# Hash attention before a SwiGLU block: all hash products in 32 columns, signs written once and spread, the late ones moved behind the row sums

## The chip, the core and the metric

The kernel runs on one NeuronCore of one Trainium2 chip. The metric is the device time of one execution in microseconds (us). The core has a matrix engine (TensorE, "PE" in the profile, with its weight loads as "PEld"), VectorE ("DVE"), ScalarE ("ACT"), GpSimd ("POOL") and SyncE ("SP"). Each engine carries out its own instructions in order. DMAs are issued by SP, ACT and POOL queues ("SPq", "ACTq", "POOLq") and carried by 16 shared DMA engines.

## What is computed

```python
# q, k, v: (4, 8, 768, 64), proj: (64, 6)
q_bits = (einsum('bhsd,dk->bhsk', q, proj) > 0)
k_bits = (einsum('bhsd,dk->bhsk', k, proj) > 0)
q_bucket = sum(q_bits * 2**arange(6), axis=-1)       # k_bucket likewise
mask = q_bucket[:, :, :, None] == k_bucket[:, :, None, :]
scores = where(mask, q @ k.T / 8, -1e9)
attn = softmax(scores)
x = (attn @ v).transpose(0, 2, 1, 3).reshape(3072, 512)
g = x @ w_gate                                       # (512, 1536)
out = (g * sigmoid(g) * (x @ w_val)) @ w_out         # (1536, 512)
```

Two tokens attend to each other only if the signs of all six hash products agree.

## The kernel before

**Pairs and units.** The 32 heads are handled two at a time: a pair n (0 to 15) is one batch and two heads, and head h of the pair lies in partitions 64h to 64h+63. A pair has two halves of 384 query columns, and a half has six chunks c of 128 keys. The main loop (L729) takes one half per turn: six times `score` (L448), then six times `attend` (L460), with `add` (L478) summing the exponentials on VectorE between scores.

**The mask as a product.** For each head, `score` adds two products in PSUM (L451 to L456): the one of the fp32 operands `T["k"]`, `T["q"]`, for both heads, and then the one of the bf16 operands `bits["k"]`, `bits["q"]` (tiles `kb`, `qb`), again for both heads. The bits are the signs of the hash products. The ones of k are multiplied by 2^34, with a constant row, so that a key with any other sign falls by a huge number and its exponential is zero. The operand rows of head 0 are partitions 0 to 63, those of head 1 are 64 to 127.

**The steps that prepare a pair.** `front(n)` (L369) returns a list of steps for pair n. For pairs 0 to 4 these are four transposes on TensorE, each with a ScalarE copy (`transpose`, L372), and four hash products (`hash_bits`, L392), each with a full 128-column weight `hash_w` in which the 32 hash columns stand twice, at columns 0 and 64. Each gives all 128 rows, so one ScalarE sign (L387) writes both heads, and for k one VectorE multiplication (L389) follows. `prepare_pair` (L717) runs steps, and `finish(rest)` runs the multiplications they leave behind. For pairs 1 to 4 the transposes of pair n+1 are issued in the first half of pair n, the two k products in the second half behind the scores (L750), and the two q products behind the attends (L760). The next instructions of TensorE are the scores of pair n+1.

For pairs 5 to 15 the transposes are done on VectorE, and `hash_blocks` (L398) issues four products of 32 columns into four groups of 32 PSUM partitions, with weights `hash_w[:, 0:32]`. A sign is then taken twice, once to partitions 0 to 31 and once to 64 to 95, and for k each is multiplied separately. These steps are `chores` (L769), handed out one for each unit of size of the feed-forward pieces (`atoms`, L780): size 1 for an up product (L625), size 2 for a down product (L690). The first chore of a second half is nothing, the second is `hash_blocks`, so that two up products stand between it and what is ahead of it.

**The row sums.** `total(n)` (L489) multiplies the sums of exponentials by `ones` in four 32-column products (L500, tile `sum`), takes a reciprocal on VectorE (L508), and issues eight SP transfers (L513) of 32 x 384 fp32 that spread it over partitions. `norm` (L518) then scales `xT`. For pairs 0 to 3 `total` is issued in the next pair, behind its second score; for later pairs at the end of the second half.

**The SP queue.** At the end of a second half `load(n + 2)` (L757) issues q, k and v of that pair on SP. v has two buffers, so the one of pair n+2 waits for the attends of pair n.

**The weights.** During the first quarter of the time VectorE and ScalarE turn the feed-forward weights from doubles to fp32 (`narrow`, L285) and form sums of blocks (`form`, L310). `prepare_on` hands these out four and three steps per half. GpSimd loads the words (L263) and moves formed blocks to and from DRAM (L308, L318, L320, L329).

Of the kernel before, what the change touches and what calls it, by code (L numbers as in the profile page):

```python
# [8 lines left out]
FP32 = mybir.dt.float32  # L9
# [3 lines left out]
ALU = mybir.AluOpType  # L13
AF = mybir.ActivationFunctionType
# [4 lines left out]
def kernel(  # L19
# [11 lines left out]
    nc = tc.nc  # L31
# [38 lines left out]
    def bank(name):  # L70
        return banks.tile([P, 512], FP32, tag="ps", name=name)
# [68 lines left out]
    HR = 16  # L140
    assert NBITS + 1 <= HR and 2 * HR == BLOCK
    rules = wraw.tile([P, PIECE, 2], I32, tag="words", name="rules").rearrange("p f w -> p (f w)")
    rules = rules.bitcast(FP32)[:, 0 : 2 * P].rearrange("p (x r) -> p x r", r=P)

    nc.gpsimd.memset(rules[:, 0, :], -(2.0**-120))
    nc.gpsimd.memset(rules[:, 1, :], 0.0)
    groups = rules.rearrange("p x (g r) -> p x g r", r=HR)
    nc.gpsimd.memset(groups[:, 0, :, NBITS : NBITS + 1], 1.0)
    for h in range(2):
        g = groups[:, 1, h * D // HR + h, :]  # L150
        nc.gpsimd.memset(g[:, 0:NBITS], OFF / 2)
        nc.gpsimd.memset(g[:, NBITS : NBITS + 1], -NBITS * OFF / 2)
    nc.vector.tensor_tensor(rules, rules, ident.unsqueeze(1).to_broadcast([P, 2, P]), op=ALU.mult)
    columns = konst.tile([P, 2], FP32, tag="columns", name="columns")
    nc.vector.tensor_reduce(out=columns, in_=rules, axis=AX.X, op=ALU.add)
    nudge, times_k = (columns[:, x : x + 1] for x in range(2))

    hash_w = konst.tile([P, P], FP32, tag="hash", name="hash")
    nc.vector.memset(hash_w, 0.0)
    for h in range(2):  # L160
        rows = slice(h * D, (h + 1) * D)
        nc.vector.tensor_copy(hash_w[rows, h * HR : h * HR + NBITS], two_proj[rows, :])
    nc.vector.tensor_copy(hash_w[:, D : D + BLOCK], hash_w[:, 0:BLOCK])
    ones = konst.tile([P, BLOCK], FP32, tag="ones", name="ones")
    nc.gpsimd.memset(ones, 1.0)

# [4 lines left out]
    for i in range(RING):  # L171
        t = konst.tile([P, 2, AW], FP32, tag=f"A{i}", name="A")
        nc.gpsimd.memset(t[:, :, HQ:AW], 1.0)
        ring.append(t)

# [176 lines left out]
    def prepare_on(n):  # L354
        for _ in range(n):
            next(preparing, None)
# [12 lines left out]
    def front(n):  # L369


        def transpose(name, half):  # L372
            if (name, n) not in T:
                T[name, n] = opnd.tile([P, S], FP32, tag=name + "T", name=name + "T")
            ps = bank("tps")
            for i in range(CH):
                nc.tensor.transpose(ps[:, i * P : (i + 1) * P],
                                    raws[name, n][:, half * CH + i, :, :].rearrange("p h d -> p (h d)"),
                                    ident)
            nc.scalar.copy(T[name, n][:, half * HQ : (half + 1) * HQ], ps[:, 0:HQ])  # L380

        bits["q", n] = sides["q", n % 2]
        bits["k", n] = sides["k", n % 2]

        def sign(name, half, to, ps):
            o = bits[name, n][to, half * HQ : (half + 1) * HQ]
            nc.scalar.activation(o, ps, AF.Sign, bias=nudge[to])  # L387
            if name == "k":
                return lambda: nc.vector.tensor_scalar(o, o, scalar1=times_k[to], scalar2=None,  # L389
                                                       op0=ALU.mult)  # L390

        def hash_bits(name, half):  # L392
            ps = bank("hps")
            nc.tensor.matmul(ps[:, 0:HQ], hash_w, T[name, n][:, half * HQ : (half + 1) * HQ],  # L394
                             start=True, stop=True)
            return [sign(name, half, slice(0, P), ps[:, 0:HQ])]

        def hash_blocks():  # L398

            tile_ = bank("hps")  # L400
            for i, (name, half) in enumerate((name, half) for name in "kq" for half in range(2)):
                nc.tensor.matmul(tile_[i * BLOCK : (i + 1) * BLOCK, 0:HQ],  # L402
                                 hash_w[:, 0:BLOCK], T[name, n][:, half * HQ : (half + 1) * HQ],
                                 start=True, stop=True)

            def evict(name, half):
                i = 2 * (name == "q") + half
                ps = tile_[i * BLOCK : (i + 1) * BLOCK, 0:HQ]
                for to in (0, D):
                    scale = sign(name, half, slice(to, to + BLOCK), ps)  # L410
                    if scale:
                        more.append(scale)

            more = []
            return [lambda at=at: evict(*at) for at in
                    (("k", 0), ("k", 1), ("q", 0), ("q", 1))] + [lambda: [f() for f in more] and None]

        def transpose_blocks(name):
            T[name, n] = opnd.tile([P, S], FP32, tag=name + "T", name=name + "T")
            nc.vector.transpose(T[name, n], raws[name, n].rearrange("p c h d -> p (c h d)"))  # L420

        if n > NP:

            return [lambda name=name: transpose_blocks(name) for name in "qk"] + [hash_blocks]
        order = [("k", 0), ("k", 1), ("q", 0), ("q", 1)]
        turns = [lambda x=x: transpose(*x) for x in order]
        hashes = [lambda x=x: hash_bits(*x) for x in order]
        if n == 0:
            return [turns[0], turns[2], hashes[0], hashes[2], turns[1], hashes[1], turns[3],
                    hashes[3]]  # L430
        return turns + hashes


    units = [(n, half, c) for n in range(len(pairs)) for half in range(2) for c in range(NCH)]
# [282 lines left out]
    def prepare_pair(count):  # L717
        for _ in range(count):
            rest.extend(f for f in steps.pop(0)() or [] if f)

    def finish(todo):
        while todo:
            todo.pop(0)()

    prepare_pair(4)
    finish(rest)
    N = len(units)
    credit = 0.0
    for u in range(0, N, NCH):  # L729
        n, half, _ = units[u]  # L730
        gating = u >= LATE
        if u == MOVE:
            progress["late"] = True
            for t in late_ring:
                nc.gpsimd.memset(t[:, :, HQ:AW], 1.0)
        for c in range(NCH):
            score(u + c)
            if u == 0 and c in (0, 1, 2, 4):
                prepare_pair(1)
                finish(rest)  # L740
            if c == 1 and half == 0 and 0 < n <= NP:
                total(n - 1)
            if c:
                add(u + c)
        if n <= NP:
            finish(waiting)
        if not gating and half == 0:
            steps = front(n + 1)
        if not gating and u > 0:
            prepare_pair(2)  # L750
        for _ in range(1 if u else 2):
            scale_ahead()
        for c in range(NCH):
            attend(u + c)
        if not gating:
            scale_ahead()
        if half == 1 and n + 2 < len(pairs):  # L757
            load(n + 2)
        if not gating:
            prepare_pair(2 if u > 0 else 4)  # L760
        finish(first)
        finish(rest)
        prepare_on(0 if u == LATE else 4)
        if half == 1 and n >= NP:
            total(n)
        prepare_on(0 if LATE - NCH <= u <= LATE else 3)
        if not gating:
            continue
        chores = []  # L769
        if n + 1 < len(pairs):  # L770
            if half == 0:
                steps = front(n + 1)
                chores = [None, steps.pop(0), None, steps.pop(0)]
            else:
                chores = [None, steps.pop(0)]

        credit += 14 if n < 2 * NP else 15.75
        end = True
        part = 0
        while atoms and (credit > 0 or not end):  # L780
            size, atom, end = atoms.pop(0)
            credit -= size
            atom()
            part += size
            if part >= 11 or u + NCH == N and part >= 6:
                finish(waiting)
                if u + NCH == N:
                    finish([first.pop(0) for _ in range(min(2, len(first)))])
            if 5 < part < 14 if u == LATE else part < 9:
                prepare_on(size)  # L790
            if 6 < part < 11 or u == LATE and part > 10:
                scale_ahead()
            for _ in range(size):
                if chores:
                    step = chores.pop(0)
                    chores.extend(step and step() or [])
        while chores:
            step = chores.pop(0)
            chores.extend(step and step() or [])
# [34 lines left out]
```

The softmax here doesn't subtract the row's maximum and nothing guards it: scores larger than these inputs give would overflow.

## Time and profile before

| | |
|---|---|
| median of 3 runs | 1008.99 us (1008.4 to 1009.31) |
| the profiled execution | 1007.17 us |
| its span, first to last instruction | 1005.4 us |
| PE busy | 999.8 us (99%) |
| DVE busy | 574.7 us (57%) |
| ACT busy | 417.4 us (42%) |
| hash products, 128 columns (L394) | 40 of them |
| hash products, 32 columns (L402) | 88 of them |
| signs of 32 x 384 (L387) | 88, mean 569 to 573 ns |
| v loads on SP (L81) | 16 of 384 KB, median 3.3 us from issue to landing |

An fp32 product stands in the trace as two matmul instructions. The kernel's TensorE instructions are pipelined, so a row's mean duration of a matmul (490 ns for 384 columns) is longer than the distance to the next one; the chain of waits, which lays instructions end to end, gives the distances. The span falls into two parts. Up to some 119.5 us there is attention of pairs 0 to 4 with the weights prepared beside it; from there on attention and feed-forward products alternate (the weights are all prepared by about 290 us), and attention ends at about 802 us.

### The profile page before, as it was taken

The page shows a single profiled execution, that of the slowest core. Times are in us where ns is not written, and L with a number is a line of the kernel's source. Part 1 is how long each engine was busy: PE and PEld are TensorE (multiplying, and loading weights), DVE is VectorE, ACT ScalarE, POOL GpSimd, SP SyncE. Part 2 cuts the span into 40 slices and gives each one's busy share as a digit, 9 for nine tenths or more (in the row PEclk, how much of TensorE's full clock was granted, in tenths as well). Part 3 has the DMA queues.
Part 4 walks back from the last instruction along what each step waited for, and adds up shares of the span by engine and source line. Part 5 has one row for each costly group of instructions (what it writes and reads, how often), then busy time and mean ns, then how long its engine had stood idle before and what let it go on. Part 6 is the DMA issues. An engine that isn't in the chain of part 4 may idle for free.

```text
span 1005.4 us, 12486 instructions
## 1 busy us (share of the span) xinstructions
PE 999.8 (99%) x4597; PEld 603.9 (60%) x4597; DVE 574.7 (57%) x919; ACT 417.4 (42%) x921; POOL 98.7 (10%) x192
## 2 busy tenths in 40 slices
PE   9999999999999999999999999999999999999998
PEld 4444455555576775555557776555555787555687
DVE  4788898887883624556464543545557342435421
ACT  7777457575424215335351323435444201222200
POOL 2222132231000000000000000000000000111000
PEclk9999999999999999999999999999999999999999
DMA  7777495886213032433331304242122011323101
GB/s 229 200 257 228 145 243 156 229 279 169 76 39 78 22 95 67 101 97 92 95 105 28 72 17 115 76 102 84 54 85 78 22 37 63 105 76 113 32 27 37
DMA packets 120029, 106.21 MB, mean 106 GB/s; under 512 B 89024, under 2 KB 103360, under 8 KB 119968
## 3 DMA queue, kind: packets, MB, share of 16 engines
q0 software_dynamic: 19104, 73.28, 22.8%
q1 hardware_dynamic: 100064, 31.94, 14.0%
q8 instruction: 36, 0.59, 0.3%
q10 hardware_dynamic: 800, 0.20, 0.1%
q14 instruction: 25, 0.20, 0.1%
HBM read 81.79 MB, written 17.30 MB: 99 GB/s over the span
## 4 chain that ended last, share of the span: by engine, by line
PE 89%; DVE 7%; SPq 2%; issue 1%; DMA 1%; DVEq 0%; ACT 0%
PE up L544 42%; PE po L544 21%; PE sc L455 12%; PE av L469 10%; SPq L513 2%; DVE acc L487 1%; PE sum L500 1%; DVE wo L508 1%; PE hps L402 1%; DMA wo<-wo 1%; DVE room L294 1%; PE hps L394 1%; DVE room L326 0%; DVE room L349 0%; DVE xT L520 0%
## 5 line engine op out<-in xcount | busy, mean ns | idle before, releaser
L544 PE MATMUL up<-xT,room 128*128 128x384 f32 x768 | 263.7, 490 | 0.4 <-DVE xT L520 0.4
L544 PEld LDWEIGHTS up<-xT,room 128*128 128x128 f32 x768 | 144.2, 190 | 110.3 <-issue 15.4
L544 PE MATMUL up<-xc,room 128*128 128x384 f32 x576 | 197.4, 487 | 0.0
L455 PE MATMUL sc<-qT,kT 64*128 64x384 f32 x768 | 160.3, 494 | 0.0
L544 PEld LDWEIGHTS up<-xc,room 128*128 128x128 f32 x576 | 109.7, 191 | 76.0 <-ACT hid L607 0.2
L548 DVE TENSOR_TENSOR c<-c,up 128x384 f32<-128x384 f32 x72 | 39.8, 553 | 179.7 <-PE up L544 178.5
L487 DVE TENSOR_TENSOR acc<-acc,A 128x768 f32<-128x768 f32 x128 | 122.7, 958 | 15.4 <-ACT A L458 2.6
L308 POOL DMA_DIRECT2D room<-ram x96 | 51.9, 541 | 717.9 <-PE up L544 710.3
L458 ACT ACTIVATE A<-sc 128x384 f32<-128x384 f32 x256 | 105.4, 505 | 4.9 <-PE sc L455 4.7
L679 ACT COPY o<-po 128x256 f32<-128x256 f32 x48 | 17.9, 372 | 196.5 <-PE po L544 196.5
L455 PEld LDWEIGHTS sc<-qT,kT 64*128 64x128 f32 x768 | 68.0, 187 | 50.7 <-issue 43.3
L469 PE MATMUL av<-A,vraw 128*64 128x384 f32 (+1 forms) x512 | 88.2, 487 | 0.0
L530 ACT ACTIVATE th<-c 128x384 f32<-128x384 f32 x72 | 37.6, 523 | 110.9 <-DVE c L531 83.4
L548 DVE TENSOR_TENSOR o<-o,po 128x256 f32<-128x256 f32 x36 | 15.1, 421 | 111.6 <-PE po L544 82.4
L458 ACT ACTIVATE room<-sc 128x384 f32<-128x384 f32 x128 | 54.4, 495 | 33.6 <-PE sc L455 33.6
L544 PE MATMUL po<-wo,hid 128*128 128x256 f32 x288 | 66.9, 382 | 0.0
L544 PE MATMUL po<-wo,room 128*128 128x256 f32 x288 | 66.6, 381 | 0.2 <-DVE room L548 0.2
L544 PE MATMUL po<-room,hid 128*128 128x256 f32 x288 | 66.1, 380 | 0.0
L607 ACT COPY c<-up 128x384 f32<-128x384 f32 x72 | 34.4, 478 | 74.5 <-PE up L544 74.3
L455 PE MATMUL sc<-qb,kb 64*128 64x384 bf16 x384 | 65.2, 323 | 0.0
L469 PEld LDWEIGHTS av<-A,vraw 128*64 128x64 f32 x512 | 36.8, 137 | 46.0 <-issue 45.4
L544 PEld LDWEIGHTS po<-wo,hid 128*128 128x128 f32 x288 | 54.2, 190 | 12.0 <-issue 4.9
(109 smaller groups left out, 998.3 us busy)
## 6 DMA issues: line engine op xcount, KB each, us to landing
room<-ram POOLq DMA_DIRECT2D x48, 512.0 KB, 4.7
room<-ram POOLq DMA_DIRECT2D x48, 384.0 KB, 3.9
vraw<-in_v_dram SPq DMA_DIRECT2D x16, 384.0 KB, 3.3
ram<-room POOLq DMA_DIRECT2D x12, 512.0 KB, 4.7
out_dram<-o SPq DMA_DIRECT2D x48, 128.0 KB, 1.7
room<-in_moe_w_out_dram POOLq DMA_DIRECT2D x10, 512.0 KB, 6.7
qraw<-in_q_dram SPq DMA_DIRECT2D x48, 96.0 KB, 3.1
hid<-in_moe_w_gate_dram POOLq DMA_DIRECT2D x9, 512.0 KB, 6.2
```

Source lines behind the costliest of these rows:

```text
L294: nc.vector.scalar_tensor_tensor(out=wi, in0=hi, scalar=-(1 << 31), in1=wi, op0=ALU.bitwise_and, op1=ALU.bitwise_or)
L308: nc.gpsimd.dma_start(places[k % 2][:, PARTS[go], :], ram[k % NG][:, PARTS[go], :])
L455: nc.tensor.matmul(sc[h], x["k", n][rows, ks], x["q", n][rows, qs], start=start, stop=not start)
L458: nc.scalar.activation(weights(u)[:, h, 0:HQ], sc[h], AF.Exp, scale=SCALE)
L469: nc.tensor.matmul(ps[h * D : (h + 1) * D, 0:width], raws["v", n][:, h, c, :], a[:, h, 0:width], start=c == 0, stop=c == NCH - 1)
L487: nc.vector.tensor_tensor(acc[n, half], acc[n, half], a[:, :, 0:HQ], op=ALU.add)
L513: nc.sync.dma_start(t[at : at + BLOCK, half, :], r[g : g + BLOCK, :])
L530: nc.scalar.activation(th, g, AF.Tanh, scale=0.5)
L544: nc.tensor.matmul(ps, a, x, start=start and i == 0, stop=i == len(pairs_) - 1, skip_group_check=True)
L548: nc.vector.tensor_tensor(o, a, b, op=op)
L607: nc.scalar.copy(tile_of(g, spot), c)
L679: nc.scalar.copy(o, c)
```

## The change

1. `hash_w` has 32 columns instead of 128; every hash product goes through `hash_blocks(todo, own)`, which puts up to four of them side by side in one PSUM tile.
2. A sign is taken once, to partitions 0 to 31. `spread` then makes partitions 64 to 95: for k by two VectorE multiplications over all columns of `todo` (high from low, then low in place), for q by a VectorE copy in pair 0 and by one transfer on the SP queue in all other pairs.
3. The scale for k becomes two columns; three of the bits tiles are cleared by GpSimd at the start, as partitions 32 to 63 and 96 to 127 are no longer written.
4. Pairs 1 to 4: one step with all four products stands behind the second score of the second half of the pair before; its `spread` is run by the `finish(rest)` behind the attends and behind `load(n + 2)`.
5. Pairs 5 to 15: the four products are issued right behind `total(n)`; the four signs and `spread` are chores.
6. Pair 0: k and q of the first half are hashed together before the first score, those of the second half together behind the third score.

```diff
-    hash_w = konst.tile([P, P], FP32, tag="hash", name="hash")
+    hash_w = konst.tile([P, BLOCK], FP32, tag="hash", name="hash")
...
-    nc.vector.tensor_copy(hash_w[:, D : D + BLOCK], hash_w[:, 0:BLOCK])
...
+    for t in (sides["k", 0], sides["q", 0], sides["q", 1]):
+        nc.gpsimd.memset(t, 0.0)
...
+        def hash_blocks(todo, own):
             tile_ = bank("hps")
+            for i, (name, half) in enumerate(todo):
+                nc.tensor.matmul(tile_[i * BLOCK : (i + 1) * BLOCK, 0:HQ], hash_w,
+                                 T[name, n][:, half * HQ : (half + 1) * HQ],
                                  start=True, stop=True)
+            low, high = slice(0, BLOCK), slice(D, D + BLOCK)
+
+            def sign(i, name, half):
+                nc.scalar.activation(bits[name, n][low, half * HQ : (half + 1) * HQ],
+                                     tile_[i * BLOCK : (i + 1) * BLOCK, 0:HQ], AF.Sign, bias=nudge)
+
+            def spread():
+                for name in "kq":
+                    hs = [half for x, half in todo if x == name]
+                    b = bits[name, n][:, hs[0] * HQ : (hs[-1] + 1) * HQ]
+                    if name == "k":
+                        for to, times in ((high, times_k[1]), (low, times_k[0])):
+                            nc.vector.tensor_scalar(b[to], b[low], scalar1=times, scalar2=None,
+                                                    op0=ALU.mult)
+                    elif own:
+                        nc.vector.tensor_copy(b[high], b[low])
+                    else:
+                        nc.sync.dma_start(b[high], b[low])
+
+            return [lambda i=i, at=at: sign(i, *at) for i, at in enumerate(todo)] + [spread]
+
+        def hash_at_once(todo, own=False):
+            *signs, spread = hash_blocks(todo, own)
+            for f in signs:
+                f()
+            return [spread]
...
+        order = [("q", 0), ("q", 1), ("k", 0), ("k", 1)]
         if n > NP:
+            return ([lambda name=name: transpose_blocks(name) for name in "qk"]
+                    + [lambda: hash_blocks(order, False)])
         turns = [lambda x=x: transpose(*x) for x in order]
         if n == 0:
+            return [turns[2], turns[0], lambda: hash_at_once([("k", 0), ("q", 0)], True),
+                    turns[3], turns[1], lambda: hash_at_once([("k", 1), ("q", 1)], True)]
+        return turns[2:] + turns[:2] + [lambda: hash_at_once(order)]
...
-            if u == 0 and c in (0, 1, 2, 4):
+            if u == 0 and c < 3 or not gating and half == 1 and c == 1:
                 prepare_pair(1)
-                finish(rest)
+                if u == 0:
+                    finish(rest)
...
-        if not gating and u > 0:
+        if not gating and half == 0 and u > 0:
             prepare_pair(2)
...
-        if not gating:
+        if not gating and half == 0:
             prepare_pair(2 if u > 0 else 4)
         finish(first)
         finish(rest)
         prepare_on(0 if u == LATE else 4)
+        chores = []
         if half == 1 and n >= NP:
             total(n)
+            if n + 1 < len(pairs):
+                chores = [None] + steps.pop(0)()
```

More of the change, by code (lines that the diff above doesn't have):

```diff
@@ L142 @@
     rules = wraw.tile([P, PIECE, 2], I32, tag="words", name="rules").rearrange("p f w -> p (f w)")
-    rules = rules.bitcast(FP32)[:, 0 : 2 * P].rearrange("p (x r) -> p x r", r=P)
+    rules = rules.bitcast(FP32)[:, 0 : 3 * P].rearrange("p (x r) -> p x r", r=P)
     nc.gpsimd.memset(rules[:, 0, :], -(2.0**-120))
-    nc.gpsimd.memset(rules[:, 1, :], 0.0)
+    nc.gpsimd.memset(rules[:, 1:3, :], 0.0)
     groups = rules.rearrange("p x (g r) -> p x g r", r=HR)
@@ L149 @@
     for h in range(2):
-        g = groups[:, 1, h * D // HR + h, :]
+        g = groups[:, 1 + h, h, :]
         nc.gpsimd.memset(g[:, 0:NBITS], OFF / 2)
         nc.gpsimd.memset(g[:, NBITS : NBITS + 1], -NBITS * OFF / 2)
-    nc.vector.tensor_tensor(rules, rules, ident.unsqueeze(1).to_broadcast([P, 2, P]), op=ALU.mult)
-    columns = konst.tile([P, 2], FP32, tag="columns", name="columns")
+    nc.vector.tensor_tensor(rules, rules, ident.unsqueeze(1).to_broadcast([P, 3, P]), op=ALU.mult)
+    columns = konst.tile([P, 3], FP32, tag="columns", name="columns")
     nc.vector.tensor_reduce(out=columns, in_=rules, axis=AX.X, op=ALU.add)
-    nudge, times_k = (columns[:, x : x + 1] for x in range(2))
-    hash_w = konst.tile([P, P], FP32, tag="hash", name="hash")
+    nudge, *times_k = (columns[0:BLOCK, x : x + 1] for x in range(3))
+    hash_w = konst.tile([P, BLOCK], FP32, tag="hash", name="hash")
     nc.vector.memset(hash_w, 0.0)
@@ L383, in front @@
         bits["k", n] = sides["k", n % 2]
[L385 to L396, printed above, removed]
@@ L398, in hash_blocks @@
-        def hash_blocks():
+        def hash_blocks(todo, own):
             tile_ = bank("hps")
-            for i, (name, half) in enumerate((name, half) for name in "kq" for half in range(2)):
-                nc.tensor.matmul(tile_[i * BLOCK : (i + 1) * BLOCK, 0:HQ],
-                                 hash_w[:, 0:BLOCK], T[name, n][:, half * HQ : (half + 1) * HQ],
+            for i, (name, half) in enumerate(todo):
+                nc.tensor.matmul(tile_[i * BLOCK : (i + 1) * BLOCK, 0:HQ], hash_w,
+                                 T[name, n][:, half * HQ : (half + 1) * HQ],
@@ L404, in hash_blocks @@
                                  start=True, stop=True)
[L406 to L416, printed above, removed]
+            low, high = slice(0, BLOCK), slice(D, D + BLOCK)
@@ L420, in transpose_blocks @@
             nc.vector.transpose(T[name, n], raws[name, n].rearrange("p c h d -> p (c h d)"))
+        order = [("q", 0), ("q", 1), ("k", 0), ("k", 1)]
         if n > NP:
-            return [lambda name=name: transpose_blocks(name) for name in "qk"] + [hash_blocks]
-        order = [("k", 0), ("k", 1), ("q", 0), ("q", 1)]
+            return ([lambda name=name: transpose_blocks(name) for name in "qk"]
+                    + [lambda: hash_blocks(order, False)])
         turns = [lambda x=x: transpose(*x) for x in order]
-        hashes = [lambda x=x: hash_bits(*x) for x in order]
         if n == 0:
-            return [turns[0], turns[2], hashes[0], hashes[2], turns[1], hashes[1], turns[3],
-                    hashes[3]]
-        return turns + hashes
+            return [turns[2], turns[0], lambda: hash_at_once([("k", 0), ("q", 0)], True),
+                    turns[3], turns[1], lambda: hash_at_once([("k", 1), ("q", 1)], True)]
+        return turns[2:] + turns[:2] + [lambda: hash_at_once(order)]
     units = [(n, half, c) for n in range(len(pairs)) for half in range(2) for c in range(NCH)]
@@ L723, in finish @@
             todo.pop(0)()
-    prepare_pair(4)
+    prepare_pair(3)
     finish(rest)
@@ L768 @@
             continue
[L769 to L775, printed above, removed]
+        if n + 1 < len(pairs) and half == 0:
+            steps = front(n + 1)
+            chores = [None, steps.pop(0), None, steps.pop(0)]
         credit += 14 if n < 2 * NP else 15.75
```

## The prediction

> **What bounds the kernel now.** I read the page first, then the chain of waits in order of time, the rows of the hash tile, the queues' own waits, and the time from issue to landing of single DMAs.
>
> ```profile
> PE 999.8 (99%) x4597; PEld 603.9 (60%) x4597; DVE 574.7 (57%) x919; ACT 417.4 (42%) x921; POOL 98.7 (10%) x192
> PE   9999999999999999999999999999999999999998
> DVE  4788898887883624556464543545557342435421
> DMA  7777495886213032433331304242122011323101
> ```
>
> TensorE hardly ever waits: 5.6 us of 1005.4 are idle, so time taken off its queue is gained unless something else is then late. But in the first 119.5 us VectorE and the DMA engines are full as well. There the chain runs through them:
>
> ```profile
> 108.90 2.48 DVE wo L508
> ...
> 111.39 0.56 SPq L513
> ...
> 116.12 2.02 DMA wo<-wo
> ...
> 118.46 1.03 DVE xT L520
> ...
> 119.53 0.59 PE up L544
> ```
>
> That is the last of four such stretches, one for each pair: reciprocal, eight SP transfers, landing, norm. TensorE idles only 0.4 us before 119.53. Two chains of equal length, then: a shorter TensorE queue alone gains little there, a longer one costs all of it. After 119.5 TensorE alone sets the pace:
>
> ```profile
> 143.70 0.78 PE sum L500 x8
> 144.48 2.78 PE up L544 x8
> 147.26 0.78 PE hps L402 x8
> 148.04 15.68 PE up L544 x48
> ```
>
> An undisturbed run of 56 up instructions takes 18.26 us, so 8 cost 2.61 and 48 cost 15.65. The four 32-column hash products cost 0.78 and with the edges around them 2.78 + 0.78 + 15.68 - 18.26 = 0.98 us. Four of 128 columns stand in the chain as two stretches of 1.49 us, at 26.65 and 32.16.
>
> Now the place where the change puts a transfer, the border from pair 1 to pair 2. TensorE, and the SP queue (start, length):
>
> ```profile
> 55.86 1.56 PE L394 MATMUL hps<-qT,hash 128*128 128x384 f32 x4
> 55.99 0.37 SPq L81 DMA_DIRECT2D vraw<-in_v_dram  x1
> 57.34 0.92 PE L455 MATMUL sc<-qT,kT 64*128 64x384 f32 x4
> 58.13 0.34 PE L455 MATMUL sc<-qb,kb 64*128 64x384 bf16 x2
> ```
>
> The attends end at 55.86, and v of pair 3 is issued 0.13 us later, since SP waits for them. The SP queue's waits say so, and the DMA view of 55 to 57 us gives that load's landing:
>
> ```profile
> SPq L81 <- PE av L469: 168.2, 14, 22.0
> vraw<-in_v_dram SPq DMA_DIRECT2D x1, 384.0 KB, 9.7
> ```
>
> 9.7 us from issue to landing. The same view at the borders at 32.2, 79.8 and 104.3 us gives 3.2, 6.5 and 5.4: GpSimd's weight loads fill the DMA engines there (six of them are issued between 52.7 and 56.4).
>
> [...] the SP queue's packets of that v load run from 60 to 65.5 us, and a 48 KB SP copy issued at 64.27 lands 4.5 us later, after it, while its lowest landing is 1.8. [...]
>
> **The change part by part.**
>
> *Early products, pairs 1 to 4.* Before: 2.98 us of TensorE each. After: 0.98. The k pair's 1.49 behind the scores becomes 0.98 within them (0.51 less); the q pair's 1.49 behind the attends goes.
>
> *Signs inside the scores.* Four signs of 0.57 us (L387, 32 x 384) now stand on ScalarE between the exponentials of chunk 1 and chunk 2: 2.3 us ahead of four pairs of exponentials of some 0.85. Scores take two of seven PSUM banks each, so chunk 5 waits for the exponential of chunk 2. In pair 1: scores start at 45.30, copies of qT end at 47.04, exponentials of 0 and 1 at 48.6, signs at 50.9, exponential 2 at 51.7; chunk 5 would otherwise begin at about 50.7. I take a wait of 0.9 us; bounds 0 (ScalarE catches up during the hash) and 1.5. With the 0.51 saved, the attends end 0.4 later than before. In pair 0 ScalarE still has all four copies, and I add 0.4 there.
>
> *The q transfer, pairs 1 to 4: the step that decides.* `finish(rest)` stands behind `load(n + 2)`. So the copy of qb is issued behind a v load that itself waits for the last attend[...]. Queued behind the wait: on SP this copy; on TensorE everything, because the second head's bits product of chunk 0 needs it, and TensorE is in order. It gets there 0.81 us after the attends (two fp32 products 0.65, one bits product 0.16). The copy lands, with L the landing of v, at 0.13 + L + 0.3. The 0.3 is an estimate, for 48 KB beside v's 384 KB; bounds 0 and 1. TensorE idles L - 0.38. Before, 1.49 us of hash stood in this place, so each border loses L - 1.87, and with the 0.4 above L - 1.5. Landings: 3.2 + 9.7 + 6.5 + 5.4 = 24.8, so 18.8 us. At the last two borders the crowding loads follow VectorE, which falls about 2 us less behind than TensorE (its reciprocal waits 1.6 us in the queue at 60.1 to 61.7 today), so v meets fewer of them: up to 4 us off; I take 2. That leaves 16.8. VectorE can't shorten this: its next reciprocal needs the sum behind chunk 1.
>
> *Clock.* Idle stretches of 2.8, 9.3, 6.1 and 5.0 us[...]. I take 2 in all; bounds 0 and 5.
>
> *VectorE, early.* Two multiplications of 32 x 768 in place of two of 128 x 384. The row has 0.31 us for 384 columns[...], at most 0.62. That is +0.2 to +0.7 us a pair. While TensorE waits it hides in that wait; if that cover is gone it adds about 1.5 us in all.
>
> *Late products, pairs 5 to 15.* Right behind `sum`, of the same column shape, they share its edges: 0.98 becomes 0.65 (two passes of 0.327) to 0.78. I take 0.25 gained each, bounds 0 and 0.33: 11 x 0.25 = 2.8 us. The bank is no obstacle: today's hash starts at 203.62, before the reciprocal of the same pair is done with `sum` at 204.15, so it takes another one. Signs fall by four and multiplications by two a pair, on engines at 42% and 57%: nothing, covered by TensorE. Their SP copy has the rest of the 14 pieces (at least 10 us) before the next scores; uncovered it would cost 2 to 3 us a pair.
>
> *Start.* Pair 0 has four products in two groups: 3.2 us become about 1.5, but chunk 3 then waits for signs and multiplications behind the third score, and the first score for a copy. Gain 0.2; bounds -1 and +1. GpSimd's three clears take about 0.4 us each (0.20 for 128 x 128), inside its 5.5 us of idle before 9.35; uncovered about 1.2. The `rules` work is a few 0.1 us under the wait for inputs.
>
> Sum: 16.8 + 0.4 + 2 - 0.2 - 2.8 = +16.2 us on the profiled 1007.17 (span 1005.4 and 1.8 around it): 1023.4. The median of the runs shown is 1.8 above that execution, so 1025.
>
> **Rivals.**
>
> *The copy is not held up by v.* If its packets pass, it lands 2.3 us after issue as the `wo` copies do (median of 32): 0.13 + 0.37 + 0.1 + 2.3 = 2.9 us behind the attends against 2.3 when the old bits product began. Each border then costs 0.6 + 0.4, four of them 4, less 3.0: about 1010. For it: this copy is small. Against: v's packets moved only from 60 us on, so the engines were full whatever the order.
>
> *Faster.* The copy lands at the 1.8 us minimum and ScalarE causes no bank wait. Then each border is even, 0.5 us a pair is kept, and the late gain is full: -4 x 0.5 - 11 x 0.33 - 0.2 = -5.8, 1003. It decides at a landing of the copy within 2.3 us of the last attend. Against it: VectorE's own chain, which grows by 0.2 to 0.7 a pair and has no slack, and the four measured landings of v. If VectorE keeps its pace this becomes about 1007, no change.
>
> *More waits than counted.* All landings in full, three slow clocks and 1 us behind v: 18.8 + 0.4 + 5 + 2.8 - 1 = +26, 1035.
>
> **How the numbers follow.** The forecast (1016 to 1030) has 0.68, more waits 0.10, the passing copy 0.12, the even case 0.04, faster 0.06. A difference of 0.2% (2 us) is about what a measurement of this kernel can tell from no change. Of the passing copy's share 0.02 falls within that. Faster 0.06, same 0.06, slower 0.88. The range reaches from the passing copy, 1010, to the upper bound, 1035.
>
> **What would show it.** Right: in the changed trace the first bits product of pairs 1 to 4 waits for a DMA into qb, 3 to 9 us each, longest for pair 2; that copy lands just behind v; the up product that waits for norm, at 119.53 today, near 138.7; then per pair about 0.25 us less, with sum and hps adjacent. Wrong: bits waits under 1 us, a copy that lands before v, or idle TensorE inside the late pairs.

## The result, and the profile after

| | before | after |
|---|---|---|
| median | 1009.15 us (4 runs, 1008.4 to 1010.29) | 1033.26 us (4 runs, 1031.49 to 1034.24) |
| ratio of the runs | | 1.0236 (95% interval 1.0218 to 1.0254): slower |
| profiled execution, span | 1007.17, 1005.4 us | 1032.78, 1030.9 us |

The page of the changed kernel, engine totals and rows of tenths:

```profile
PE 1000.6 (97%) x4597; PEld 602.8 (58%) x4597; DVE 575.8 (56%) x900; ACT 393.8 (38%) x877; POOL 101.7 (10%) x195
PE   9866989999999999999999999999999999999998
PEclk9989899999999999999999999999999999999999
```

TensorE has become idle in slices two, three, four and six and slow-clocked in slices three and five, so within 26 to 155 us, and nowhere else (PEclk is the granted clock, the share of full speed that TensorE was allowed). Its waits name the cause (total, times, longest; `sc` is the tile of the scores):

```profile
PE sc L458 <- DMA qb<-qb: 23.0, 4, 8.7
PE sc L458 <- DVE kb L406: 1.3, 3, 0.7
PE idle L134 <- DVE kb L131: 1.3, 1, 1.3
PE sc L458 <- ACT kb L397: 0.9, 4, 0.2
```

Four waits, one for each of pairs 1 to 4, on the copy that makes the high half of qb. At the border from pair 1 to pair 2, the SP queue (start, length), and then the DMA view of 55 to 64 us (last column: us from issue to landing):

```profile
61.05 0.37 SPq L81 DMA_DIRECT2D vraw<-in_v_dram  x1
61.52 1.15 SPq L411 DMA_DIRECT2D qb<-qb  x1
```

```profile
vraw<-in_v_dram SPq DMA_DIRECT2D x1, 384.0 KB, 8.5
qb<-qb SPq DMA_DIRECT2D x1, 48.0 KB, 8.6
```

The copy is issued 0.47 us behind v and lands about 0.6 us after it. The landings of v at the four borders are 3.3, 8.5, 9.0 and 4.5 us, those of the copy 3.0, 8.6, 9.2 and 4.2. The chain of waits, which ran through reciprocals and VectorE in this part of the kernel before, now goes through the copy:

```profile
56.97 4.07 PE av L472 x24
...
61.52 8.56 DMA qb<-qb
...
70.13 2.08 PE sc L458 x7
72.20 1.48 PE sum L503 x8
...
73.71 2.57 DVE wo L511
```

The eight sum instructions take 1.48 us here and took 0.78 in the late pairs before. The windows of 2 us around that border (busy PE, PEld, DVE, ACT, POOL, then granted clock, DMA share, GB/s) show why:

```profile
62.00:64.00 2.00, 0.32 (x1) 0.07 (x2) 1.93 (x4) 1.04 (x3) 0.00 (x0) 1.00 0.96 377
64.00:66.00 2.00, 0.00 (x0) 0.00 (x0) 1.83 (x4) 0.00 (x0) 0.00 (x0) 0.74 1.02 415
...
68.00:70.00 2.00, 0.00 (x0) 0.00 (x0) 0.00 (x0) 0.00 (x0) 1.47 (x2) 0.50 1.04 382
70.00:72.00 2.00, 1.87 (x7) 0.86 (x6) 0.00 (x0) 0.49 (x1) 0.00 (x0) 0.50 0.98 363
72.00:74.00 2.00, 2.00 (x12) 0.63 (x12) 0.29 (x1) 0.88 (x2) 0.00 (x0) 0.50 0.10 33
74.00:76.00 2.00, 2.00 (x12) 0.86 (x12) 2.00 (x1) 0.54 (x2) 0.00 (x0) 0.70 0.00 0
```

The granted clock falls to 0.50 while TensorE is idle and stays there for some 5 us after the copy has landed (at 70.08). The late pairs, in the chain of the changed kernel:

```profile
171.68 0.78 PE sum L503 x8
172.46 0.65 PE hps L391 x8
173.11 18.26 PE up L547 x56
```

The four hash products cost 0.65 us behind the sums, and the 56 up instructions take the 18.26 us of an undisturbed run: 0.33 gained of 0.98 in each pair.

**A ledger** of the profiled execution against the one of before, at the first up product behind the attends of pair 4's first half (115.67 before, 144.29 after, so 28.6 us late):

| part | us |
|---|---|
| start, to the first attend (16.06 to 17.12) | +1.1 |
| second halves of pairs 0 to 3, first score to first attend: 6.54 became 7.13, 7.01, 7.03, 7.03 | +2.0 |
| idle for the copy, 2.61 + 7.81 + 8.74 + 3.80 = 22.96, less the four q hashes of 1.49 that stood there | +17.0 |
| slow clock behind the four waits | +7.8 |
| rest (0.15 of it a wait for kb at 61.98) | +0.7 |
| from there to the end | -3.1 |

The slow clock is what the stretch from the bits product that waited to the start of chunk 3 has grown by: 4.34, 5.13, 5.12 and 4.23 us at the four borders, against 2.75 at full clock (experiment e4). The 8.3 us in the expectations below is another count of the same thing, half the time at half clock after work resumed.

Of the last row, 0.6 us is the wait for norm at 119.53 in the kernel before, which is gone: VectorE caught up while TensorE waited. The late pairs give 2.5. From the row sums of one pair to those of the next it takes 0.33 to 0.43 us less in ten of the eleven steps (56.43 became 56.10 in most), but the step from pair 5 to pair 6 takes 0.9 more (57.19 became 58.13).

### The profile page after: what moved, and what is told of

Read it like the earlier page. It is cut to its first block, busy times and chain, and to the rows that moved or that the text cites. A ratio compares the mean times of both kernels' runs of the same rounds, so it can differ in the third digit from the quotient of the medians.

```text
span 1030.9 us, 12453 instructions
## 1 busy us (share of the span) xinstructions
PE 1000.6 (97%) x4597; PEld 602.8 (58%) x4597; DVE 575.8 (56%) x900; ACT 393.8 (38%) x877; POOL 101.7 (10%) x195
## 4 chain that ended last, share of the span: by engine, by line
PE 90%; DMA 4%; DVE 2%; ACT 2%; SPq 1%; issue 1%; POOL 0%; DVEq 0%; ACTq 0%
PE up L547 41%; PE po L547 21%; PE sc L458 13%; PE av L472 11%; DMA qb<-qb 2%; PE sum L503 1%; SPq L516 1%; PE hps L391 1%; DMA words<-in_moe_w_out_dram 1%; DVE wo L511 1%; DMA wo<-wo 1%; ACT kb L397 0%; ACT A L461 0%; PE idle L134 0%; PE tps L378 0%
## 5 line engine op out<-in xcount | busy, mean ns | idle before, releaser
L547 PE MATMUL up<-xT,room 128*128 128x384 f32 x768 | 260.9, 488 | 0.0
L458 PE MATMUL sc<-qT,kT 64*128 64x384 f32 x768 | 168.9, 508 | 1.5 <-ACT kb L397 0.9
L458 PEld LDWEIGHTS sc<-qT,kT 64*128 64x128 f32 x768 | 70.2, 191 | 84.3 <-issue 72.9
L458 PE MATMUL sc<-qb,kb 64*128 64x384 bf16 x384 | 69.6, 329 | 24.3 <-DMA qb<-qb 23.0
L533 ACT ACTIVATE th<-c 128x384 f32<-128x384 f32 x72 | 37.6, 523 | 127.7 <-DVE c L534 88.5
```

Source lines behind the costliest of these rows:

```text
L458: nc.tensor.matmul(sc[h], x["k", n][rows, ks], x["q", n][rows, qs], start=start, stop=not start)
L533: nc.scalar.activation(th, g, AF.Tanh, scale=0.5)
L547: nc.tensor.matmul(ps, a, x, start=start and i == 0, stop=i == len(pairs_) - 1, skip_group_check=True)
```

## The experiments

**The copy on VectorE (e1).** In `front`, for pairs 1 to 4:

```diff
-        return turns[2:] + turns[:2] + [lambda: hash_at_once(order)]
+        return turns[2:] + turns[:2] + [lambda: hash_at_once(order, True)]
```

> The changed kernel with one thing undone: for pairs 1 to 4 the high half of qb is made by a VectorE copy, as in pair 0, and not by an SP transfer. If the transfer behind v is the cause, the four waits (23.0 us in all) shrink to under 0.5 us each, the four slow-clock stretches (8.3 us) go, and what is left is the start (+1.1), the signs within the scores (+2.0), VectorE's larger work and the late gain (-3.2 to -3.6): 1006 to 1010 us. If the signs within the scores or VectorE's work are what costs, it stays at 1020 us or more.

Measured 1011.32 us, ratio to before 1.0025 (1.0014 to 1.0036). Of the 24.1 us lost, 21.9 are back; a little more is left than I expected. The waits for qb are gone, but kb is now waited for (5.1 us), and the chain is VectorE's again:

```profile
114.24 2.48 DVE wo L511
...
121.64 1.90 DMA wo<-wo
...
123.87 1.03 DVE xT L523
124.89 0.04 issue
124.94 1.24 PE up L547 x3
```

The last norm of this part starts at 123.87, and at 118.46 in the kernel before. So the 32-column products for pairs 1 to 4 win nothing even without the transfer: VectorE's work is longer there (the two multiplications take 0.85 us and the copy 0.35, in place of 0.54), and it sets the end. Its four reciprocals start 1.9, 3.0, 4.4 and 5.4 us later than before. The longer work is about 0.7 of the 1.1 us that each pair adds; the rest isn't traced.

**The transfer ahead of the loads (e2).** In the main loop:

```diff
+        if half == 1 and not gating:
+            finish(rest)
         if half == 1 and n + 2 < len(pairs):
             load(n + 2)
```

> The changed kernel with the transfer kept on SP, but issued ahead of the loads of pair n+2 and not behind them. If it is the place in the SP queue (behind a v load that waits for the attends) that costs, the copy is issued as soon as the signs are there, some 6 us before the attends end, lands before TensorE needs it, and the time is 1006 to 1010 us. If small transfers are slow there wherever they stand, because the DMA engines are full, waits of several us stay and the time is over 1018 us.

Measured 1008.43 us, ratio 1.0 (0.9991 to 1.0008). The SP queue of this kernel at the second border:

```profile
49.55 0.51 SPq L411 DMA_DIRECT2D qb<-qb  x1
...
56.44 0.37 SPq L81 DMA_DIRECT2D vraw<-in_v_dram  x1
```

The same copy is issued 6.9 us ahead of v and lands 1.9 us later; the four copies take 1.9, 1.9, 1.9 and 3.0. No wait for it is left. The place in the queue is the cause: two added lines take back what the change lost. That it only equals before, with 2.2 us gained in the late pairs, agrees with VectorE's chain: its four reciprocals start 1.4, 1.7, 2.5 and 3.0 us later than before, and TensorE waits 5.5 us for kb. The last norm is 3.9 us late; the 1.0 beyond the reciprocal's delay comes with the row-sum transfers, which this time are issued right behind a v load (113.92 and 114.61).

**Another queue at the same place (e3).**

```diff
-                        nc.sync.dma_start(b[high], b[low])
+                        (nc.scalar if n <= NP else nc.sync).dma_start(b[high], b[low])
```

> The changed kernel with the copy of pairs 1 to 4 on ScalarE's DMA queue, at the same place behind the attends: [...]the same full DMA engines. If ring order behind v is what delays it, it lands 2 to 4.5 us after issue, the four waits sum to 6 to 10 us, and the time is 1010 to 1018 us. If the backlog of GpSimd's loads on the engines delays it, it lands 4 to 9 us after issue at the second and third border as before, the waits stay at 18 to 23 us, and the time is 1027 to 1034 us.

Measured 1027.48 us, ratio 1.0187 (1.0169 to 1.0206), on the edge of the second expectation, and the waits lie between the two:

```profile
PE sc L458 <- DMA qb<-qb: 16.5, 4, 5.2
```

The copy lands 3.5, 5.7, 5.8 and 5.0 us after issue. At the two crowded borders that is 2.9 and 3.4 us sooner than behind v, but still 3.8 us slower than on quiet engines (1.9 in e2 at the second border, where the DMA share from 49 to 51 us is 9.7%). At the other two it is no sooner, and the waits there, 2.66 and 4.13 us, are no shorter than the 2.61 and 3.80 of the changed kernel. So the order within v's queue, the ring order of the expectation, is less than half of the delay at the crowded borders: 2.9 of the 6.7 us by which the copy was later than those 1.9, and 3.4 of 7.3. The rest is the full DMA engines, and the packets by queue show whose. In this run, from 61 to 62 us, with v (61.13) and the copy (61.39) both issued, only GpSimd's queue moves packets, with 100.4% of the 16 engines' time, and from 55 to 66 us it moves 2.79 MB, SP's 0.09 and ScalarE's 0.04. In the changed kernel GpSimd's queue alone moves packets from 61.52, where the copy is issued, to 65.0 us, with 95.7%. That is 3.5 of the copy's 8.6 us. (At the first border it is v: from 33 to 35 us of e3 only the SP queue moves any, 12 packets, and in the changed kernel from 34.3 to 35.9, with 58.0%.) Both causes hold at the crowded borders, and neither alone explains the delay.

**A busy TensorE in the wait (e4).** In `score`, in the bits loop, ahead of the second head's product of chunk 0:

```diff
+    warm = konst.tile([P, 512], BF16, tag="warm", name="warm")
+    nc.gpsimd.memset(warm, 0.0)
...
+                if h == 1 and not start and c == half == 0 and 0 < n <= NP:
+                    ps = bank("warm")
+                    for _ in range((11, 34, 38, 16)[n - 1]):
+                        nc.tensor.matmul(ps, warm[:, 0:P], warm, start=True, stop=True)
```

> The changed kernel with products of zeros added ahead of the bits product that waits at each of the four borders (11, 34, 38 and 16 of 512 columns, about the length of each wait), so that TensorE is busy while it waits. They add work and take nothing away. If the slow stretch behind each wait is the clock that falls when TensorE idles, the 8.3 us behind the waits go and the time falls to 1024 to 1028 us. If those products are slow for another reason (the transfer still running, the memory in contention), the time stays at 1032 to 1035 us.

Measured 1025.56 us, ratio 1.0171 (1.0156 to 1.0186): 7.7 us less than the changed kernel, with 99 products more. TensorE at the second border:

```profile
60.33 7.51 PE L463 MATMUL warm<-warm 128*128 128x512 bf16 x34
69.15 0.32 PE L465 MATMUL sc<-qb,kb 64*128 64x384 bf16 x1 [1.30 <-DMA qb<-qb]
69.15 0.96 PE L465 MATMUL sc<-qT,kT 64*128 64x384 f32 x4
69.90 0.37 PE L465 MATMUL sc<-qb,kb 64*128 64x384 bf16 x2
70.20 0.85 PE L510 MATMUL sum<-acc,ones 128*32 128x384 f32 x8
...
71.90 0.81 PE L465 MATMUL sc<-qT,kT 64*128 64x384 f32 x4
```

The copy still lands 9.7 us after issue. From the bits product to chunk 3 it is 2.75 us (69.15 to 71.90), not 5.13, and the mean granted clock of the run is 1.000. The other three borders give 2.75, 2.75 and 2.77. The slow stretch was the clock, and taking these stretches as full speed gives the 7.8 us of the ledger. That the medians differ by as much, 7.7, is in part luck: in the profiled executions e4 is 6.8 us shorter, with copies that land 1.1 and 0.6 us later at the crowded borders and a start that happens to be 0.5 us shorter.

**The late move alone (e5)**, on the kernel before:

```diff
+        chores = []
         if half == 1 and n >= NP:
             total(n)
+            if n + 1 < len(pairs):
+                chores = [None] + steps.pop(0)()
...
-                chores = [None, steps.pop(0)]
```

> The kernel before with one part of the change alone: for pairs 5 to 15 the four 32-column hash products stand right behind the row sums; signs are still taken twice, nothing else differs. If products of the same column shape share their edges, each pair gains 0.33 us of TensorE (0.98 to 0.65), 11 of them 3.6 us, and TensorE sets the pace there: 1005.5 us against 1009 of before, a ratio near 0.9965. If the changed kernel's late gain came from fewer signs and multiplications instead, the time is that of before.

Measured 1005.86 us, ratio 0.9968 (0.9956 to 0.9981): faster than both kernels. Its chain in a late pair:

```profile
145.02 0.78 PE sum L500 x8
145.80 0.65 PE hps L402 x8
146.45 18.26 PE up L544 x56
```

**The whole late part (e6)**, with the steps of pairs 0 to 4 as before: 128-column weights and `hash_bits` come back for them, and so do their places in the main loop. Of that edit, only the lines that return the steps of pairs 1 to 4:

```diff
...
-        return turns[2:] + turns[:2] + [lambda: hash_at_once(order)]
+        return turns + hashes
...
```

> The changed kernel's late part (signs once, two wide VectorE multiplications, an SP transfer for q, products behind the sums) with the steps of pairs 0 to 4 as before. If the late transfer and the fewer signs are hidden behind TensorE, it equals the kernel with the moved products alone: 1005.5 us, within 1 us of it. If the late transfer is needed before it lands, or the fewer signs free something, it differs by 2 us or more.

Measured 1006.12 us, ratio 0.9973 (0.9963 to 0.9983), the same as the move alone within their intervals. One sign in place of two, the wide multiplications and the late transfer neither cost nor give anything that shows.

**Less TensorE work alone (e7)**, on the kernel before:

```diff
         def hash_bits(name, half):
+            if name == "q" and 2 <= n <= NP:
+                return []
```

> The kernel before without the q hash products and their signs for pairs 2 to 4 (left out; the bits of q are those of an earlier pair): 3 x 1.49 = 4.5 us less on TensorE and 3.5 us less on ScalarE, nothing less on VectorE. If VectorE's chain is as long as TensorE's in that part, it gains less than 1.5 us. If TensorE alone bounds it, it gains 4 to 4.5 us: 1004.6 us.

Measured 1008.59 us, ratio 0.9997 (0.9989 to 1.0006). Three times 1.49 us gone from TensorE give nothing; they turn into waits for VectorE:

```profile
PE sc L457 <- DVE kb L389: 3.8, 3, 1.8
...
PE av L471 <- DVE wo L510: 1.3, 2, 0.8
PE up L546 <- DVE xT L522: 0.6, 1, 0.6
```

## Why the prediction was right

**The step that decides** was named rightly: the copy issued behind `load(n + 2)`, TensorE in order behind it (at the second border it is busy for 0.00 us from 64 to 70), pair 2 waiting long, a copy that lands about with v. The idle time was predicted as the sum of L - 0.38 with 22.8 us of landings, 21.3 us; measured 22.96. That it came so close is in part luck: v's landing at the third border did not get shorter, as I assumed with 2 us off; it went from 6.5 to 9.0, while the second went from 9.7 to 8.5 and the fourth from 5.4 to 4.5. The four make 25.3, and the longest wait was pair 3's (8.74), not pair 2's. What makes the copy late was half right. The place behind v on SP is proved by e2 (landings of 1.9 to 3.0 us ahead of it), but the order within that queue, on which I had rested the copy's delay, is less than half of it at the crowded borders by e3 (2.9 of 6.7 us, 3.4 of 7.3); the rest is the backlog of GpSimd's loads on the engines, which I had named as what makes v slow but for the copy had used only as an argument against the first rival.

**The term that was mis-sized** is the clock: "I take 2 in all; bounds 0 and 5". It was 7.8 by the trace and 7.7 by e4, outside its bounds, and what it exceeds the forecast's 2 by is most of the gap from 1025 to 1033. Nothing measured stood behind the 2: TensorE of the kernel before waits for 1.3 us at most, at a mean granted clock of 1.000, so what a longer wait does to the clock was not shown, and the term was my estimate. The traces of the change show two things that it did not cover. A wait of 2.61 us was enough: the clock fell at about 37.6 us, just after work had resumed. And the slow clock outlasted the wait: at the second border it rose at about 75.2, 5 us after work had resumed at 70.13, which cost 2.4 us. All four waits had such a loss, 1.6, 2.4, 2.4 and 1.5 us. The last section gives the times of all eight changes of the clock.

**Signs within the scores**: +2.0 us predicted (four times 0.4 and 0.4 more for pair 0), 2.0 measured (0.6 and three times 0.5).

**The start**: -0.2 predicted with bounds of 1, +1.1 measured. Little of it can be put on the change: in e5, whose code for pair 0 is that of before, the first attend starts at 16.80 and not at 15.99 (both from the list of TensorE's instructions), because its first transposes are slow (0.84 us for three and not 0.52). They are slow in the changed kernel too (0.85). In e1 and e2, which have its code for pair 0 and quick transposes, the first attend starts at 16.3, so the change itself costs about 0.3. GpSimd's clears took 0.74 to 0.76 us each and not 0.4, still inside its idle time.

**VectorE early**: the multiplication of 768 columns is 0.408 us, against 0.310 for 384 before. My range for a pair, +0.2 to +0.7, was an estimate whose low end no trace had shown; the two take 0.85 us in place of 0.54, so +0.3. I gave 1.5 us in all if its cover were gone; e2, where it is gone, has the reciprocals 1.4 us late at the first pair and 3.0 at the fourth, so 1.6 over three pairs, and in e1, with the copy as well, the last norm is 5.4 us late.

**The late move**: -2.8 predicted, 0.25 a pair of at most 0.33. The pairs did take all of 0.33, but 11 times that is 3.6, and the row sums of pair 4 and of pair 15 are only 2.5 us closer in the changed kernel and 2.8 in e5 (median -3.0): one step, from pair 5 to pair 6, lost about 1 us against this, in e5 and e6 too. The forecast's size is right by two misses that cancel.

**Two chains of equal length**: this reading of the profile held. e7 shows it alone, and e1 and e2 show what it means for the change: the 2 us a pair that the narrow products take off TensorE for pairs 1 to 4 could not become time.

**The signs named.** The waits for a DMA into qb are there, 2.6 to 8.7 us, the copies land 0.2 to 0.7 us behind v, and in the late pairs sum and hps are adjacent. One did not come: no up product waits for norm any more. Of the signs of being wrong, TensorE idle inside the late pairs shows once, for 0.6 us at 250.5, in the step that lost time.

**The rivals.** The passing copy (1010) and the faster case (1003) fell: both needed a copy not held up at its place. What the faster case becomes if VectorE keeps its pace, about 1007 and no change, is near what e2 measured. On its own queue the copy still took 5.7 and 5.8 us at the crowded borders, so 1010 could not be had by another queue alone. "More waits than counted", 1035, was nearer than my forecast: its landings in full (24.8, measured 25.3) held, its 1 us behind v did not, and its 5 us of slow clock were still too few.

What stays open: how little work between two times of the grid below makes the clock fall, why the move of the late products loses 1 us once, between pairs 5 and 6, and how the 5.7 us of e3's copy divide between GpSimd's packets and v's.

## What to carry to other kernels

A transfer behind a load in a queue starts no sooner than the load may be issued (here at 61.52, behind a v load that was held until 61.05); ask what that load waits for, and who needs the small one next: the same copy cost 23 us of idle TensorE behind a v load and nothing ahead of it. Where two engines are equally long, taking work from one gave nothing here (e7, 4.5 us fewer on TensorE, ratio 0.9997), and a new wait on it cost in full (23.0 us), with the slow clock behind it on top (7.8). Put products of the same column shape next to each other: that part alone, moved, was worth 0.3% (0.98 us a pair became 0.65).

## What the runs showed of the hardware that I had not expected

A TensorE wait of 2.61 us lowered the granted clock to 0.50. The windows at the first border, in the changed kernel (the clock is the third number from the end: 1.00, 0.57, 0.50, 0.99):

```profile
36.00:37.40 1.40, 0.02 (x2) 0.02 (x2) 1.26 (x3) 0.00 (x0) 1.40 (x3) 1.00 0.70 175
37.40:39.00 1.60, 1.60 (x7) 0.62 (x6) 1.19 (x2) 0.49 (x1) 1.53 (x3) 0.57 0.84 274
39.00:41.00 2.00, 2.00 (x12) 0.60 (x12) 0.26 (x1) 0.87 (x2) 1.55 (x3) 0.50 1.06 365
41.00:43.00 2.00, 2.00 (x16) 1.10 (x16) 2.00 (x1) 1.08 (x3) 0.00 (x0) 0.99 0.94 344
```

Work resumed at 37.38, and full speed was back only at 41 us. And products of zeros that do nothing useful, put into the waits, were worth 7.7 us.

Read from the changed kernel's trace in steps of 0.1 us, the granted clock falls at 37.64, 64.94, 99.08 and 133.21 us and rises at 41.05, 75.19, 109.32 and 136.62. All eight times lie on one grid, whose step is measured as (136.62 - 37.64) / 29 = 3.413 us (0, 8, 18 and 28, and 1, 11, 21 and 29 steps after 37.64), whenever TensorE stops or resumes. In the steps of this grid that end with the first two falls TensorE still worked for 0.8 and 0.6 us, in those that end with the other two not at all. The steps in which it worked for 1.6 us, after resuming at 70.13 and 104.29, did not bring full speed back; the next, busy throughout, did, and so did one busy for 3.1 us. In e4, waits of up to 1.30 us left the clock at 1.000. So here the loss depends on where in the grid work resumes. As an estimate from these times it is half the time that is then still spent at half clock, 3.4, 5.1, 5.0 and 3.1 us, or 8.3 in all, against 7.8 measured.
